# Attention's sink columns copied by another engine, the sums' addition moved the other way, and the last block's remainder behind a later slot

## The chip, the cores and the metric

One NeuronCore of a Trainium2 chip runs the kernel. The metric is the device time of one execution in microseconds. Before the change it is 624.29 us, the median of 3 runs (624.04 to 624.83).

The core has a matrix engine (PE, with its weight loads as PEld), a vector engine (DVE), a scalar engine (ACT), a general engine (POOL, also called GpSimd) and a queue that issues most DMAs (SP). Each engine works through its own instructions in program order and waits on semaphores of the others.

## The reference: what is computed

Three stages follow one another. The first is attention with a window and sinks, for batch 2, 8 heads, 768 positions and 64 columns a head; a position sees the last 128 positions and the first 4 (the sinks):

```python
keep = is_sink | in_window
scores = np.where(keep, scale * q @ k.T, -1e9)
a = np.exp(scores - max(scores))
a = a / (np.sum(a, axis=-1, keepdims=True) + 1e-09)
x = a @ v
```

The second is a layer of 512 to 2048 to 512 with a rational function between its products, the third one of the same size with the square of a ReLU:

```python
h = x @ w_in
P = a[0] + a[1] * h + a[2] * h**2 + a[3] * h**3
Q = 1.0 + abs(b[0]) * abs(h) + abs(b[1]) * h**2
x = (P / (Q + 1e-6)) @ w_out
h = np.maximum(x @ w_in2, 0.0)
out = (h * h) @ w_out2
```

There are 1536 tokens in all. The weights come as 64-bit floats.

## The kernel before, in words

**Attention** goes by blocks of 128 positions: `u` from 0 to 11, six to a batch (`NB`). A block has 4 head pairs, and two steps `m`, each with two pairs; `NM` is 24. `step(m)` writes out by hand, in program order, what every engine does: `scores` (PE's products, then DVE's masked copy L368 and a reduction L375 with its accumulator), `expo` (ACT's exponentials L392, whose accumulators give the row sums `rs`), `trans` (PE transposes the probabilities, ACT copies them from PSUM, POOL splits them into two triangles at L433 and L437), `pv` (PE, into the bank `O`).

The sinks are 8 columns for each head, 64 in a block. In an even step, between the first and the second pair's `scores`, stand `sinks(u - 1)` and `sums(u - 1)`. The first copies these columns from the probabilities `pe` to the tile `sr` (L401, DVE; the first block of a batch, 0 and 6, has none). The second adds 1e-9 to the row sums in place (L408, ACT) and writes their reciprocals to the next 8 columns of `sr` (L409, DVE). `sinks_t` transposes `sr` on PE (L413); in the odd step `sinks_and_sums` multiplies it with the sinks' values (L465) and spreads the reciprocals (L469), and `result` multiplies the block's output with them (L475, DVE, tile `xf`).

`parts_of(u)` splits a finished block into two parts for the layers' products: ACT casts it (`xh`, L482), POOL subtracts (`xl`, L483). It stands two blocks later, in the even step behind the second `scores`; for the last block, 11, it stands at the end of the last step.

**The layers** go by slots. A step `k` of the layers is a chunk of 512 tokens and a piece of 128 of the 2048 columns; `slot(k)` has, in program order, for ACT and POOL the split of step `k - 2` (`act_c`: `gh` at L653, `gl` at L654), the conversion of weights that are ready (`w_fin`, L273 and L274), DVE's rest of step `k - 1` (`act_b`: the cubic L621, which gives a PSUM bank `T` back, ACT's logarithm and exponential L638 and L639, then L642, L644, L646), PE's first product of step `k + 1` (`g1`, L592), ACT's and POOL's start of step `k` (`act_a`, L608 to L613), weight conversion steps until `due(k)` (`w_until`, three DVE instructions a tile: L240, L246, L252), and PE's second product of step `k - 2` (`g2`, L671). Slots 0 and 1 are issued inside `attention`, with the last two steps of attention (24 and 25) between their parts; slots 2 and on by a loop behind it. The last block lies in the third chunk, whose first step is `k = 8`.

The conversion has a scratch bank and a switch: `conv["tag"]` names the PSUM bank, `U` in attention and `O` later, and `conv["on"]` is off from step 24 until attention has been issued. In between, attention's memory pool `ap` is closed and the pool `wp2` for more weights opened in its place; `wpool` says in which pool a weight tile lies.

Tiles that matter here: `sr` has two buffers, `rs` three, `xf` two, the bank `T` two, `O` one.

Of the kernel before, what the change touches and what calls it, by code (L numbers as in the profile page):

```python
# [11 lines left out]
ACTF = mybir.ActivationFunctionType  # L12
ALU = mybir.AluOpType
# [24 lines left out]
def kernel(  # L38
# [13 lines left out]
    nc = tc.nc  # L52
# [4 lines left out]
    NU = B * NB  # L57
# [33 lines left out]
    eps = cst.tile([P, 1], F32, name="eps")  # L91
# [45 lines left out]
    def setup_rest(rel, win, snk, tmp, m_1, m_2, tri):  # L137
        def addm_s(dst, src):
            nc.scalar.activation(out=dst, in_=src, func=ACTF.Identity, scale=BIG, bias=nbig)

        nc.vector.tensor_scalar(out=tri, in0=rel[:, P:], scalar1=0.0, scalar2=None, op0=ALU.is_lt)
        nc.gpsimd.tensor_tensor(out=tmp, in0=win[:, 0:P], in1=win[:, P:], op=ALU.add)
        nc.gpsimd.tensor_tensor(out=win[:, P:P + SK], in0=snk[:, 0:SK], in1=win[:, 0:SK], op=ALU.subtract)
        yield
        addm_s(m_1[:, SK:], tmp)
        nc.scalar.activation(out=win[:, P:P + SK], in_=win[:, P:P + SK], func=ACTF.Relu)
        addm_s(m_1[:, 0:SK], win[:, P:P + SK])
        yield
        addm_s(m_2[:, SK:], tmp)
        addm_s(m_2[:, 0:SK], snk[:, 0:SK])  # L150
# [26 lines left out]
    conv = {"tag": "U", "on": True}  # L177
# [12 lines left out]
    for j, (kind, m) in enumerate(jobs):  # L190
        n = 1 if kind == "v" else 1 + (wtiles[m][::2] == (0, 0)) if kind == "w" else WS + (m >= LATE)
# [73 lines left out]
    def w_fin():  # L265
        m = wst["fin"]
        if m not in wx or len(spare) <= keep[0] or int(spare[0][1:]) >= len(wpool):
            return
        wst["fin"] += 1
        xf = wx.pop(m).bitcast(F32)  # L270
        tag = spare.pop(0)
        t = wpool[int(tag[1:])].tile([P, 2, DM], F32R, tag=tag, name="w")
        nc.scalar.copy(out=t[:, 0], in_=xf)  # L273
        nc.gpsimd.tensor_tensor(out=t[:, 1], in0=xf, in1=t[:, 0].bitcast(F32), op=ALU.subtract)  # L274
        W[wtiles[m]] = (t[:, 0], t[:, 1], tag)
# [9 lines left out]
    def ps_t(tag=None, tail=False):  # L285
        if tail:
            return ps_s()[:, 0]
        if tag is None:
            tag = "U" if hq else "T"
        return ps.tile([P, 512], F32, tag=tag, name=tag, bufs=2 if tag == "T" else 1)  # L290


    def attention(ap, extra):
# [46 lines left out]
        def sink_keys(u):  # L340
            nc.gpsimd.tensor_copy(
                keys[:, :, :, P:], keys[:, :, u % NB, 0:SK].unsqueeze(2).to_broadcast([P, NPR, NB, SK])
            )
# [54 lines left out]
        def sinks(u):  # L398
            t = pe_t.pop(u)
            if u % NB:  # L400
                nc.vector.tensor_copy(  # L401
                    sr[u % 2][:, 0:HS].rearrange("p (r e s) -> p r e s", r=NPR, e=2),
                    t[:, :, :, ROW - BS:ROW - P],
                )

        def sums(u):
            rs = rs_t.pop(u)
            nc.scalar.activation(out=rs, in_=rs, func=ACTF.Identity, bias=eps)  # L408
            nc.vector.reciprocal(out=sr[u % 2][:, HS:HS + H], in_=rs)  # L409

        def sinks_t(u):
# [67 lines left out]
        def parts_of(u):  # L479
            c, t0 = u // UPC, (u % UPC) * P  # L480
            x, h = f.pop(u), xh[c][:, :, t0:t0 + P]
            nc.scalar.copy(out=h, in_=x)  # L482
            nc.gpsimd.tensor_tensor(out=xl[c][:, :, t0:t0 + P], in0=x, in1=h.bitcast(F32), op=ALU.subtract)  # L483

        NM = NU * NPR // 2
# [7 lines left out]
        def fill(d, m):  # L493

            for _ in range(m):
                nc.tensor.matmul(
                    d.rearrange("p (j n) -> p j n", n=P), lhsT=wz,
                    rhs=wz.unsqueeze(1).to_broadcast([P, 4, P]), start=True, stop=True,
                )
# [14 lines left out]
        def step(m):  # L514
            w_fin()
            nonlocal bd, moe, rest, heads
            n, (u, a) = 2 * m, divmod(m, 2)
            if m < NM:
                scores(n)
            if a == 0 and u >= 1:  # L520
                sinks(u - 1)
                sums(u - 1)
            if m < NM:
                scores(n + 1)
                if n in DENSE:
                    fill(ps_t("T"), DENSE[n])
            if m == 0:
                rest = setup_rest(*next(masks), m_1, m_2, tri)
                next(rest)
                sink_keys(0)  # L530
            if a == 0 and 2 <= u <= NU:
                parts_of(u - 2)
            if m < NM:
                expo(n)
            if m in (1, 2):
                next(rest, None)
            if 0 < m <= NM:
                trans(m - 1)
            if m == 1:
                for t in sr:  # L540
                    nc.gpsimd.memset(t, 0.0)
                bd = diagonal()
                heads = bd.rearrange("p h d -> p (h d)")
                moe = setup_moe()
            if a == 0 and u + 2 < NU:
                load(u + 2)
            if a == 0 and m < NM and u % NB == 0:
                load_sinks(u // NB)
            if m >= 5:
                next(moe, None)  # L550
                next(moe, None)
            if a == 1 and u >= 1:
                sinks_and_sums(u - 1)
            if 1 < m:
                pv(m - 2)
            if m < NM:
                expo(n + 1)
            if a == 0 and u >= 1:
                sinks_t(u - 1)
            if m == NM - 1:  # L560
                g1(0)
            if m < NM and a == 1 and u % NB == 0:
                if u:
                    sink_keys(u)
                sink_values(u // NB, bd)
            extra(m)
            if a == 1 and u >= 1:
                result(u - 1)
            if m == NM + 1:
                parts_of(NU - 1)  # L570

        for m in range(NM):
            step(m)
        for j in range(2):
            slot(j, lambda: step(NM + j))


    def part(L, g):
# [21 lines left out]
    def layers(mp, due):  # L600
# [56 lines left out]
        def g2(k):  # L657
            L, g, c, f = steps[k]
            f0, f1 = part(L, g)[0], part(L, g)[1] - 1
            if f == f0:  # L660
                acc[L, g, c] = [t[:, m] for t in [ps_s(), ps_s()] for m in range(2)]
            wo = W[L, f, 1]
            gg = gq.pop(k)
            for m in range(4):
                s = slice(m * P, (m + 1) * P)
                for a, b in ((0, 0), (0, 1), (1, 0)):
                    if L == 0:
                        lh, rh = wo[a][:, s], gg[b]
                    else:
                        lh, rh = gg[a][:, s], wo[b]  # L670
                    nc.tensor.matmul(  # L671
                        acc[L, g, c][m], lhsT=lh, rhs=rh,
                        start=(f == f0 and a + b == 0), stop=(f == f1 and a == 1),
                    )
            if c == NCH - 1:
                w_free((L, f, 1))
            if f == f1:
                done.append((L, g, c))
# [45 lines left out]

        K = len(steps)

        def slot(k, mid=None):
            if 0 <= k - 2:
                act_c(k - 2)
            w_fin()  # L730
            w_fin()
            if 0 <= k - 1 < K:
                act_b(k - 1, lambda: w_until(min(due(k), wst["int"] + 1)))
            if k + 1 < K:
                g1(k + 1)
            if k < K:
                act_a(k)
            if mid:
                cubic(st[k][1], hq[k])
                hq[k] = None  # L740
                mid()
            split_late()
            w_until(due(k))
            if 0 <= k - 2:
                g2(k - 2)
            if k == K + 1:
                finish(0)
                finish(1)
# [253 lines left out]
    EARLY = 2  # L1002
# [19 lines left out]
    slot, slots = layers(mp, due)  # L1022
    with tc.tile_pool(name="ap", bufs=1) as ap:
        NM = NU * NPR // 2

        def extra(m):
            if m == 1:
                for _ in range(NWR):
                    w_load()
            if m % 2:  # L1030
                w_until(min(WS * NA, m - 1))
            if m == NM:
                conv["on"] = False

        attention(ap, extra)
    conv["tag"], conv["on"] = "O", True
    wp2 = main.enter_context(tc.tile_pool(name="wp2", bufs=1))
    wpool += [wp2] * (NW - NA)
    for n in range(EARLY, slots):
        slot(n)  # L1040
        if n == KL + 3 * NF - 3:
            fl = verdict()
# [43 lines left out]
```

## Time and profile before

| what | value |
|---|---|
| median of 3 runs | 624.29 us |
| the profiled execution | 624.6 us |
| its span | 622.9 us |
| PE busy | 609.0 us (98%) |
| DVE busy | 434.4 us (70%) |
| ACT busy | 355.8 us (57%) |
| POOL busy | 329.2 us (53%) |
| granted clock of PE | 0.998 |

The span is what the trace covers; the rest of the execution's time lies around it. An engine's busy time is the time in which one of its instructions was running. PE's ends are modelled, so that a busy PE need not be PE at its peak. Attention lies in the first 85 us of the span, layer 1 follows to about 250 us, then layer 2.

### The profile page before, as it was taken

What the parts mean: (1) busy time and instruction counts of PE and PEld (TensorE: products, weight loads), DVE (VectorE), ACT (ScalarE), POOL (GpSimd) and SP (SyncE); (2) the same over time, 40 slices, a digit from 0 to 9 for tenths busy, and PEclk for the clock granted to TensorE, in tenths of its full rate; (3) what the DMA queues carried; (4) which work ended last, traced back from release to release, by engine and by line L of the source; (5) the groups of instructions that cost most, each with busy time, mean ns of one, the idle gap of its engine ahead of it and who ended that gap; (6) DMA issues with size and microseconds to landing.
All of it is one profiled execution on the core that took longest, in us unless ns stands there. A gap on an engine that the chain in (4) does not pass through costs nothing.

```text
span 622.9 us, 9430 instructions
## 1 busy us (share of the span) xinstructions
PE 609.0 (98%) x3317; PEld 491.1 (79%) x3317; DVE 434.4 (70%) x873; ACT 355.8 (57%) x748; POOL 329.2 (53%) x293
## 2 busy tenths in 40 slices
PE   9999999999999999999999999999999999999995
PEld 6666777788888878888888888888888888888884
DVE  5998957989989889877768879598594422441421
ACT  5999977888886877877869543243332222222210
POOL 4567655777776767666857575444352222222221
PEclk9999999999999999999999999999999999999999
DMA  8857411423332333121111447557365355500102
GB/s 232 244 146 214 120 36 35 128 87 93 98 102 78 97 97 101 38 64 35 35 34 35 115 148 256 192 176 234 131 207 198 116 191 168 175 28 1 67 1 73
DMA packets 64231, 72.03 MB, mean 116 GB/s; under 512 B 15280, under 2 KB 55216, under 8 KB 64176
## 3 DMA queue, kind: packets, MB, share of 16 engines
q1 hardware_dynamic: 64032, 71.35, 37.1%
q8 instruction: 28, 0.46, 0.3%
q14 instruction: 27, 0.22, 0.1%
q10 hardware_dynamic: 144, 0.00, 0.0%
HBM read 68.20 MB, written 3.15 MB: 115 GB/s over the span
## 4 chain that ended last, share of the span: by engine, by line
PE 65%; DVE 19%; ACT 11%; issue 2%; DMA 1%; SPq 0%; DVEq 0%; ACTq 0%
PE s L671 30%; PE T L592 23%; PE U L592 7%; DVE t L646 3%; DVE U L644 3%; ACT U L638 2%; ACT U L639 2%; ACT gh L653 2%; ACT w L273 2%; DVE t L642 2%; DVE wx L252 2%; DVE ns L375 1%; DVE O L240 1%; PE O L453 1%; PE s L363 1%
## 5 line engine op out<-in xcount | busy, mean ns | idle before, releaser
L592 PE MATMUL T<-xh,w 128*128 128x512 f32 x640 | 211.0, 391 | 0.5 <-DVE t L621 0.4
L654 POOL TENSOR_TENSOR gl<-g,gh 128x512 fp32r<-128x512 f32 x48 | 62.2, 1295 | 157.9 <-ACT gh L653 157.8
L592 PEld LDWEIGHTS T<-xh,w 128*128 128x128 f32 x640 | 120.2, 188 | 27.9 <-DVE t L621 2.7
L671 PE MATMUL s<-gh,w 128*128 128x512 f32 x384 | 126.0, 389 | 0.0
L592 PE MATMUL T<-xl,w 128*128 128x512 f32 x320 | 124.6, 389 | 0.0
L671 PE MATMUL s<-w,gh 128*128 128x512 f32 x384 | 118.1, 389 | 0.0
L274 POOL TENSOR_TENSOR w<-wx,w 128x512 fp32r<-128x512 f32 x64 | 82.7, 1293 | 7.2 <-ACT w L273 7.2
L654 POOL TENSOR_TENSOR gl<-t,gh 128x512 fp32r<-128x512 f32 x48 | 62.1, 1294 | 44.6 <-ACT gh L653 43.0
L671 PEld LDWEIGHTS s<-gh,w 128*128 128x128 f32 x384 | 72.1, 188 | 15.0
L671 PEld LDWEIGHTS s<-w,gh 128*128 128x128 f32 x384 | 72.0, 188 | 14.9
L613 POOL TENSOR_TENSOR t<-t,ah 128x512 f32<-128x512 f32 x48 | 62.2, 1296 | 37.7 <-ACT t L610 35.8
L653 ACT CAST gh<-g 128x512 fp32r<-128x512 f32 x48 | 29.9, 623 | 81.8 <-PE s L671 74.5
L671 PE MATMUL s<-gl,w 128*128 128x512 f32 x192 | 74.8, 390 | 0.9 <-POOL gl L654 0.9
L671 PE MATMUL s<-w,gl 128*128 128x512 f32 x192 | 74.7, 389 | 0.0
L592 PEld LDWEIGHTS T<-xl,w 128*128 128x128 f32 x320 | 60.1, 188 | 12.2
L653 ACT CAST gh<-t 128x512 fp32r<-128x512 f32 x48 | 29.9, 622 | 46.2 <-DVE t L646 41.9
L642 DVE SCALAR_TENSOR_TENSOR t<-t,U 128x512 f32<-128x512 f32 x48 | 33.0, 687 | 30.1 <-ACT U L639 29.5
L627 DVE TENSOR_TENSOR g<-r,T 128x512 f32<-128x512 f32 x32 | 21.8, 683 | 41.8 <-ACT r L617 41.5
L617 ACT ACTIVATE r<-T 128x512 f32<-128x512 f32 x32 | 19.2, 600 | 53.2 <-PE T L592 53.1
L392 ACT ACTIVATE pe<-ns,nmax 128x136 f32<-128x136 f32 (+1 forms) x96 | 38.3, 400 | 10.0 <-DVE nmax L375 9.6
L671 PEld LDWEIGHTS s<-gl,w 128*128 128x128 f32 x192 | 36.0, 188 | 8.8 <-POOL gl L654 1.4
L273 ACT CAST w<-wx 128x512 fp32r<-128x512 f32 x64 | 39.3, 615 | 6.4 <-DVE wx L252 6.4
(136 smaller groups left out, 1033.4 us busy)
## 6 DMA issues: line engine op xcount, KB each, us to landing
wr<-in_w_in_dram SPq DMA_DIRECT2D x54, 512.0 KB, 3.7
wr<-in_w_out_dram SPq DMA_DIRECT2D x52, 512.0 KB, 3.7
qr<-in_q_dram SPq DMA_DIRECT2D x12, 256.0 KB, 4.1
keys<-in_k_dram SPq DMA_DIRECT2D x12, 256.0 KB, 4.5
vr<-in_v_dram SPq DMA_DIRECT2D x12, 256.0 KB, 5.6
wr<-in_v_dram SPq DMA_DIRECT2D x6, 512.0 KB, 4.3
out_dram<-part SPq DMA_DIRECT2D x12, 256.0 KB, 2.0
vsc<-in_v_dram SPq DMA_DIRECT2D x2, 16.0 KB
```

Of the source, the lines that this page charges most:

```text
L273: nc.scalar.copy(out=t[:, 0], in_=xf)
L274: nc.gpsimd.tensor_tensor(out=t[:, 1], in0=xf, in1=t[:, 0].bitcast(F32), op=ALU.subtract)
L392: nc.scalar.activation(out=t[:, e, ROW - w:], in_=ns[e][:, 0:w], func=ACTF.Exp, scale=-1.0, bias=nmax[:, ix:ix + 1], accum_out=rs[:, 2 * p ...
L592: nc.tensor.matmul(h, lhsT=wi[a][:, kk * P:(kk + 1) * P], rhs=(xh, xl)[b][c][:, kk, :], start=(kk == 0 and a + b == 0), stop=(kk == KD - 1 ...
L613: nc.gpsimd.tensor_tensor(out=t, in0=t, in1=ah, op=ALU.mult)
L617: nc.scalar.activation(out=r, in_=h, func=ACTF.Relu)
L627: nc.vector.tensor_tensor(out=g, in0=st.pop(k), in1=h, op=ALU.mult)
L642: nc.vector.scalar_tensor_tensor(out=t, in0=t, scalar=QP, in1=r0, op0=ALU.add, op1=ALU.mult)
L644: nc.vector.scalar_tensor_tensor(out=r0, in0=t, scalar=-2.0, in1=r0, op0=ALU.add, op1=ALU.mult)
L653: nc.scalar.copy(out=gh, in_=g)
L654: nc.gpsimd.tensor_tensor(out=gl, in0=g, in1=gh.bitcast(F32), op=ALU.subtract)
L671: nc.tensor.matmul(acc[L, g, c][m], lhsT=lh, rhs=rh, start=(f == f0 and a + b == 0), stop=(f == f1 and a == 1),)
```

## The change

The copy of the sinks' columns is issued on ACT's queue in place of DVE's, the addition to the row sums on DVE's in place of ACT's. The split of block 11 goes from the end of the last step of attention, in slot 1, to the end of slot 2, behind its second product; slot 2 is issued inside `attention` for this, before the pool `ap` is closed. The conversion's tag and switch are set in the last step of attention, for slot 2.

```diff
         def sinks(u):
             t = pe_t.pop(u)
             if u % NB:
-                nc.vector.tensor_copy(
+                nc.scalar.copy(
                     sr[u % 2][:, 0:HS].rearrange("p (r e s) -> p r e s", r=NPR, e=2),
                     t[:, :, :, ROW - BS:ROW - P],
                 )
 
         def sums(u):
             rs = rs_t.pop(u)
-            nc.scalar.activation(out=rs, in_=rs, func=ACTF.Identity, bias=eps)
+            nc.vector.tensor_scalar(out=rs, in0=rs, scalar1=eps, scalar2=None, op0=ALU.add)
             nc.vector.reciprocal(out=sr[u % 2][:, HS:HS + H], in_=rs)
...
             if a == 1 and u >= 1:
                 result(u - 1)
-            if m == NM + 1:
-                parts_of(NU - 1)
 
         for m in range(NM):
             step(m)
         for j in range(2):
             slot(j, lambda: step(NM + j))
+        slot(2, after=lambda: parts_of(NU - 1))
...
-        def slot(k, mid=None):
+        def slot(k, mid=None, after=None):
...
             if 0 <= k - 2:
                 g2(k - 2)
+            if after:
+                after()
...
             if m == NM:
                 conv["on"] = False
+            if m == NM + 1:
+                conv["tag"], conv["on"] = "O", True
 
         attention(ap, extra)
-    conv["tag"], conv["on"] = "O", True
     wp2 = main.enter_context(tc.tile_pool(name="wp2", bufs=1))
     wpool += [wp2] * (NW - NA)
-    for n in range(EARLY, slots):
+    for n in range(EARLY + 1, slots):
         slot(n)
```

## Rows read from the trace of the kernel before

**Rows 1.** The page, engines: busy us, share of the span, instructions.
```profile
PE 609.0 (98%) x3317; PEld 491.1 (79%) x3317; DVE 434.4 (70%) x873; ACT 355.8 (57%) x748; POOL 329.2 (53%) x293
```

**Rows 2.** Busy time by stage: stretch, length, PE, PEld, DVE, ACT, POOL, clock, DMA, GB/s.
```profile
40.00:50.00 10.00, 9.10 (x118) 6.72 (x115) 9.14 (x41) 9.07 (x37) 7.08 (x9) 1.00 0.40 111
```

**Rows 3.** Waits, whole span: who waited for whom, us in total, times, longest.
```profile
PEld T L413 <- DVE sr L409: 5.9, 10, 1.2
...
PE T L413 <- DVE sr L409: 3.4, 6, 1.0
...
PEld T L592 <- DVE t L621: 2.7, 6, 0.6
...
PE s L671 <- POOL gl L654: 0.9, 1, 0.9
```

**Rows 4.** Groups by line, 0 to 140 us: busy us, mean ns | idle before.
```profile
L401 DVE COPY sr<-pe 128x64 f32<-128x64 f32 x10 | 9.2, 917 | 0.0
...
L408 ACT ACTIVATE rs<-rs,eps 128x8 f32<-128x8 f32 x12 | 3.6, 299 | 0.2
...
L415 ACT COPY st<-T 128x128 f32<-128x128 f32 x11 | 2.7, 244 | 0.0
```

**Rows 5.** DVE in order of time, attention: start us, us taken.
```profile
26.53 0.86 DVE L401 COPY sr<-pe 128x64 f32<-128x64 f32 x1
27.32 0.19 DVE L409 RECIPROCAL sr<-rs 128x8 f32<-128x8 f32 x1
...
40.01 1.24 DVE L401 COPY sr<-pe 128x64 f32<-128x64 f32 x1
...
53.40 0.20 DVE L409 RECIPROCAL sr<-rs 128x8 f32<-128x8 f32 x1
...
91.09 0.19 DVE L401 COPY sr<-pe 128x64 f32<-128x64 f32 x1
```

**Rows 6.** POOL in order of time, attention.
```profile
26.06 1.28 POOL L274 TENSOR_TENSOR w<-wx,w 128x512 fp32r<-128x512 f32 x1 [0.96 <-ACT w L273]
27.30 1.27 POOL L483 TENSOR_TENSOR xl<-xf,xh 128x512 fp32r<-128x512 f32 x1
...
39.93 1.27 POOL L483 TENSOR_TENSOR xl<-xf,xh 128x512 fp32r<-128x512 f32 x1 [1.38 <-ACT xh L482]
...
52.78 1.27 POOL L334 TENSOR_TENSOR vm<-bd,vsc 64x512 f32<-64x512 f32 x1 [2.24 <-DMA vsc<-in_v_dram]
54.01 1.27 POOL L274 TENSOR_TENSOR w<-wx,w 128x512 fp32r<-128x512 f32 x1
```

**Rows 7.** Groups by line, 0 to 140 us: DVE's `tensor_scalar` between SBUF tiles.
```profile
L118 DVE TENSOR_SCALAR su<-su 128x256 f32<-128x256 f32 x1 | 0.3, 283 | 0.0
...
L102 DVE TENSOR_SCALAR m<-su 128x128 f32<-128x128 f32 x1 | 0.2, 228 | 0.0
L134 DVE TENSOR_SCALAR su<-su,nw 128x8 f32<-128x8 f32 x1 | 0.2, 224 | 0.0
```

**Rows 8.** One line, L775: shortest/median/longest ns, first and last start us.
```profile
L775 DVE SCALAR_TENSOR_TENSOR bad<-size x1: 1261/1261/1261, 591.4 to 591.4; 128x1 f32<-128x1 f32 x1
```

**Rows 9.** POOL in order of time, layer 2.
```profile
591.32 1.31 POOL L654 TENSOR_TENSOR gl<-g,gh 128x512 fp32r<-128x512 f32 x1 [4.15 <-ACT gh L653]
```

**Rows 10.** DVE in order of time, first slots of layer 1.
```profile
95.13 0.70 DVE L644 SCALAR_TENSOR_TENSOR U<-t,U 128x512 f32<-128x512 f32 x1
95.86 0.75 DVE L646 SCALAR_TENSOR_TENSOR t<-t,fa,U 128x512 f32<-128x512 f32 x1
```

**Rows 11.** ACT in order of time, slots 1 and 2; [idle before <-releaser].
```profile
98.50 0.62 ACT L482 CAST xh<-xf 128x512 fp32r<-128x512 f32 x1 [1.23 <-DVE xf L475]
99.02 0.61 ACT L653 CAST gh<-t 128x512 fp32r<-128x512 f32 x1
```

**Rows 12.** POOL in order of time, slots 1 and 2.
```profile
99.19 1.29 POOL L483 TENSOR_TENSOR xl<-xf,xh 128x512 fp32r<-128x512 f32 x1 [2.18 <-ACT xh L482]
100.44 1.27 POOL L654 TENSOR_TENSOR gl<-t,gh 128x512 fp32r<-128x512 f32 x1
```

## The prediction

> **What bounds the kernel now.** The page first: TensorE (PE) is busy for 98% of the span [rows 1], so from layer 1 on little can be won outside it. Then the table by stage [rows 2]: between 40 and 50 us, in attention, PE, VectorE (DVE) and ScalarE (ACT) are all busy for nine tenths. Then the waits [rows 3]: what PE and its weight loads wait for is the reciprocal of L409 (3.4 us of PE, 5.9 us of loads, ten times), once the remainder `gl` of POOL (0.9 us of PE, ahead of L671), and the cubic of L621, which gives a T bank back (2.7 us of loads). These are the three places that the change can touch. Each block's chain in attention is: DVE's score reductions, the copy of the sinks' columns, the reciprocal, PE's transpose of `sr`, the next scores; DVE works nearly without a gap, so a delay there moves all that follows.
>
> **Why the copy is slow.** The copy of 128x64 takes 0.917 us on average, while ACT copies 128x128 in 0.244 [rows 4]. The lines by time say why [rows 5, 6]. The copy at 26.53 ends at 27.39; POOL's L274 runs from 26.06 to 27.34. The one at 40.01 ends at 41.25; POOL's L483 runs from 39.93 to 41.20. The one at 91.09, at the end of POOL's multiplication, takes 0.19. So the copy itself costs 0.19 and waits until POOL's running instruction has ended, and 0.05 us more.
>
> **The copy moves to ACT, the addition to DVE.** DVE loses ten copies and gets twelve additions over 128x8, in the same place of its queue: behind the reductions, ahead of the reciprocal. The question on which the sum hangs is whether the addition waits for POOL as the copy did. No row has such an addition while POOL works. The bounds: unhindered, the nearest form is L134, a 128x8 `tensor_scalar` with a per-partition scalar, 0.224 us; hindered, it ends where the copy ended. For hindered: L118 and L102 do 256 and 128 elements in 283 and 228 ns, so 128 more cost 55 ns [rows 7]. That is over two elements per ns, a rate that a DVE instruction reading one stream element by element doesn't reach: the 128x512 operations with two inputs cost 0.69 to 0.75 us [rows 10]. `tensor_scalar` between SBUF tiles thus reads through two ports, as a copy does. And smallness doesn't help: L775, one element per partition, took 1.261 us from 591.4 on while POOL ran L654 from 591.32 to 592.63 [rows 8, 9]. I take the hindered end.
>
> The Trainium skill, "SBUF — State Buffer", section "Who interferes with whom", has a rule on this that speaks against this change: copy, cast and `tensor_scalar` can all run in a mode with two ports, one of which is GpSimd's, and whichever of the two engines comes second waits until the other's whole instruction has ended. The copies above agree with it; for a `tensor_scalar` no run here shows it yet. By that rule the sum is the one below; by the 0.224 us alone it would be that of the first rival.
>
> *Full blocks.* Nine copies (blocks 1 to 5 and 7 to 10) stand in the tight part. The addition ends with POOL as the copy did, up to 0.05 us sooner because it is shorter. But the reciprocal now needs the result of the instruction just ahead on its own engine. It used to start at 27.32, 0.07 before the copy ended [rows 5]; one that needs its predecessor's result starts 0.03 after it (L644 ends at 95.83, L646 starts at 95.86) [rows 10]. So 0.10 later, less 0 to 0.05: 0.05 to 0.10 per block, I take 0.08, nine times: **+0.7 us**.
>
> *Block 6.* Blocks 0 and 6 copied nothing, but now add. In block 6 the reciprocal starts at 53.40 [rows 5], while POOL runs L334 from 52.78 to 54.05 [rows 6]. The addition would end at about 54.10, the reciprocal start 0.7 us late, with all of DVE behind it. ACT, co-critical there, saves its 0.3 us. Bounds 0 and 0.73; I take **+0.6 us**. In block 0 the pipeline is still filling and DVE waits for PE: nothing, with a second 0.7 kept for the range; in block 11 PE works on layer 1 meanwhile, which hides it.
>
> *ACT.* Twelve additions of 0.299 go, ten copies of some 0.25 come (L415 is the nearest, 0.244 for twice the columns, from PSUM [rows 4]), in the same place of its queue and with nothing awaited but ACT's own exponentials. No more than before: nothing, bounds -0.05 and +0.05 a block. PE's transpose now waits for two engines; ACT's copy stands ahead of the exponentials, done long before POOL lets the addition go.
>
> **The last block's remainder behind slot 2.** Today ACT's `xh` cast (L482) waits 1.23 us for DVE's `xf` and starts at 98.50, and `gh` of slot 0 stands behind it, at 99.02 [rows 11]. On POOL, L483 runs from 99.19, then L654 from 100.44 to 101.71 [rows 12], and for this `gl` PE waits 0.9 us. With both moved behind slot 2's second product, `gh` can start when ACT is free, at 97.27 (its input was ready at 96.61, the end of L646 [rows 10]); POOL gets it at about 97.9 and is done by 99.2, before PE asks. The stall goes: **-1.0 us** (bounds 0.9, PE's wait [rows 3], and 1.3, the L483 that goes from ahead of `gl`). ACT's logarithm and DVE's chain for slot 1 start some 1.7 us sooner too; against PE's 1.0 that is 0.7 us of lead, so the T banks come back sooner in the next slots: of the 2.7 us of load waits, of which PE shows part, **-0.7 us** (bounds 0 and 1.3). The moved cast (some 0.6) and subtraction (1.3) then stand ahead of slot 3's `gh` and `gl`, which had waited for DVE and are needed a full product later; the block's columns are read by the third chunk only, far behind. The conversions' tag and switch set earlier issue the same steps in slot 2; no DMA changes place, those of the weights follow DVE. The second weight pool opens one slot later than before, and its first tile is written in slot 4: nothing.
>
> **Sum.** +0.7 +0.6 -1.0 -0.7 = -0.4 us. The profiled execution took 624.6 (span 622.9, 1.7 around it), 0.3 above the median of 624.29; against the median the forecast is 623.9.
>
> **The rivals.**
> - *The addition doesn't wait for POOL.* Then the blocks lose the waits that PE shows behind L409: between 3.4 and 5.9 us [rows 3], some of it kept by ACT and PE, which are as busy; I take 4.2 and the tail's 1.7: 618.4. For it: a per-partition scalar may exclude the second port, and L134, too short to tell the rate, is the only row of that form. Against it: rows 5 to 9.
> - *Slower: block 6's addition loses the port twice.* Behind L334 stands L274, ready, another 1.3 us. If POOL's next instruction takes over without a gap, the addition ends 1.9 us late instead of 0.7, and if block 0 pays 0.7 as well, attention loses 0.7+1.9+0.7 = 3.3 against the tail's 1.7: 625.9. It decides from the point where POOL has two instructions back to back. Against it: at 27.3 L483 followed L274 in the same way, and the copy got through between them [rows 5, 6].
> - *The move doesn't pay.* PE finds the next wait (a T bank) in place of `gl`: the tail gives 0.4 and attention's 1.3 stay: 625.2.
>
> **How the numbers follow.** The forecast has 0.60, the free addition 0.24, the port lost twice 0.07, the unpaid move 0.09. A measurement of this kernel tells about 0.2% (1.25 us) from no change. The forecast's own range, from its bounds (-2.2 to +1.4), is 622.1 to 625.7; three twentieths of the whole lie in its part below 623.0, hardly any above 625.5. Faster: 0.24 and 0.11 of the forecast's, 0.35. Slower: 0.07, 0.03 of the unpaid move, 0.04 of the forecast's with block 0 paid in full, 0.14. Same: 0.51. The range for 8 in 10 has to reach the free addition: 618.0 to 625.5.
>
> **What would show it.** In the changed profile: additions (128x8, DVE) of 0.6 to 1.2 us on average, each ending with a POOL instruction, and PE still waiting for L409 for some 3 to 4 us; 0.22 each and that wait gone is the first rival. The block 6 reciprocal about 0.7 us later. `gl` of slot 0 issued near 98 us, no PE wait for it, fewer L592 waits for L621. PE's first product of layer 1 (L592) some 1.3 us later than now. The forecast is wrong if that product starts earlier, or if PE still stalls ahead of its first L671.

## The result, and the profile after

The changed kernel takes 628.62 us, the median of 6 runs (626.14 to 629.18), against 624.27 us before: a ratio of 1.0062, 95% interval 1.0044 to 1.008. It is slower by 4.35 us. The forecast was 623.9, with 618.0 to 625.5 as its range.

Two lines of the page of the changed kernel, to be held against before [rows 1]: PE's share has fallen, and the line of PE's clock, in tenths of full speed over 40 equal slices, which was all nines before, has a dip in the fourth and fifth slice.

```profile
PE 611.7 (97%) x3317; PEld 494.7 (79%) x3317; DVE 437.7 (70%) x875; ACT 355.8 (57%) x746; POOL 329.2 (52%) x293
...
PEclk9998899999999999999999999999999999999999
```

Now DVE in order of time (start us, us taken), to be held against [rows 5]: the additions (L408) in place of the copies, and the products L475 that end a block.

```profile
27.09 0.90 DVE L408 TENSOR_SCALAR rs<-rs,eps 128x8 f32<-128x8 f32 x1
...
40.87 1.22 DVE L408 TENSOR_SCALAR rs<-rs,eps 128x8 f32<-128x8 f32 x1
...
53.02 0.69 DVE L475 TENSOR_TENSOR xf<-O,rb 128x512 f32<-128x512 f32 x1 [0.76 <-PE O L453]
...
54.52 2.40 DVE L408 TENSOR_SCALAR rs<-rs,eps 128x8 f32<-128x8 f32 x1
56.96 0.20 DVE L409 RECIPROCAL sr<-rs 128x8 f32<-128x8 f32 x1
...
63.29 0.69 DVE L475 TENSOR_TENSOR xf<-O,rb 128x512 f32<-128x512 f32 x1 [1.74 <-ACT pe L392]
...
71.94 0.68 DVE L475 TENSOR_TENSOR xf<-O,rb 128x512 f32<-128x512 f32 x1
...
98.23 0.23 DVE L408 TENSOR_SCALAR rs<-rs,eps 128x8 f32<-128x8 f32 x1
```

And POOL in the changed kernel, to be held against [rows 6]:

```profile
26.68 1.28 POOL L274 TENSOR_TENSOR w<-wx,w 128x512 fp32r<-128x512 f32 x1 [0.95 <-ACT w L273]
27.92 1.28 POOL L483 TENSOR_TENSOR xl<-xf,xh 128x512 fp32r<-128x512 f32 x1
...
53.17 1.27 POOL L334 TENSOR_TENSOR vm<-bd,vsc 64x512 f32<-64x512 f32 x1 [1.67 <-DMA vsc<-in_v_dram]
54.41 1.26 POOL L274 TENSOR_TENSOR w<-wx,w 128x512 fp32r<-128x512 f32 x1
55.64 1.25 POOL L483 TENSOR_TENSOR xl<-xf,xh 128x512 fp32r<-128x512 f32 x1
...
97.04 1.30 POOL L612 TENSOR_TENSOR t<-t,ah 128x512 f32<-128x512 f32 x1 [2.22 <-ACT t L609]
```

The addition of 8 columns waits for POOL just as the copy did. The one at 27.09 ends at 27.99, POOL's L274 at 27.96. The one at 98.23 meets only the last 0.11 us of a POOL instruction (L612, which ends at 98.34) and takes 0.23. But in block 6 the addition comes at 54.52, just behind the start of L274 (54.41 to 55.67), and doesn't get through at that one's end: it lasts to 56.92, past the whole of L483 (55.64 to 56.89).

What that does to PE stands in PE's own lines and in the table by stage (stretch, length, PE, PEld, DVE, ACT, POOL, clock, DMA, GB/s) of the changed kernel:

```profile
54.23 0.66 PE L453 MATMUL O<-ph,vr 128*64 128x128 f32 x8
57.22 0.33 PE L413 MATMUL T<-ident,sr 128*128 128x128 f32 x1 [2.33 <-DVE sr L409]
57.48 1.57 PE L363 MATMUL s<-keys,qr 64*64 64x200 f32 x16
```

```profile
50.00:55.00 5.00, 4.88 (x68) 3.59 (x64) 4.17 (x17) 4.64 (x18) 3.33 (x6) 1.00 0.76 196
55.00:60.00 5.00, 2.73 (x21) 1.36 (x21) 4.67 (x16) 2.77 (x12) 1.89 (x2) 0.79 0.66 182
60.00:65.00 5.00, 5.00 (x35) 3.68 (x35) 3.09 (x11) 2.93 (x9) 1.50 (x3) 0.50 0.61 157
65.00:70.00 5.00, 5.00 (x49) 3.61 (x49) 3.33 (x15) 3.01 (x13) 2.20 (x3) 0.68 0.00 0
```

PE stands still for 2.33 us, and then the granted clock falls from 1.00 to 0.50, from 2.4 to 1.2 GHz. From what the three lower rows lack to 1.00, it was at half for (0.21 + 0.50 + 0.32) x 5 / 0.5 = 10.3 us. Then PE is "busy" all the time, but at half the clock.

The blocks' ends in the trace of before, for comparison:

```profile
51.89 0.69 DVE L475 TENSOR_TENSOR xf<-O,rb 128x512 f32<-128x512 f32 x1 [0.76 <-PE O L453]
...
57.83 0.68 DVE L475 TENSOR_TENSOR xf<-O,rb 128x512 f32<-128x512 f32 x1
...
65.04 0.69 DVE L475 TENSOR_TENSOR xf<-O,rb 128x512 f32<-128x512 f32 x1
```

Block 6's stretch takes 63.29 - 53.02 = 10.27 us instead of 5.94, the next one 8.65 instead of 7.21: 5.8 us more in these two.

The other part of the change did what it was forecast to do. In the changed kernel (POOL, then PE, then the waits) slot 0's `gl` (L653 here, L654 before [rows 12]) starts at 105.05, L483 of block 11 comes after it, PE goes from L591 to L670, and from the first product with `gh` to the first with `gl`, without a gap, and the load waits for the T bank are 1.1 us, 2.7 before [rows 3]:

```profile
105.05 1.29 POOL L653 TENSOR_TENSOR gl<-t,gh 128x512 fp32r<-128x512 f32 x1 [0.90 <-POOL t L612]
...
108.81 1.30 POOL L483 TENSOR_TENSOR xl<-xf,xh 128x512 fp32r<-128x512 f32 x1
110.06 1.30 POOL L653 TENSOR_TENSOR gl<-t,gh 128x512 fp32r<-128x512 f32 x1
```

```profile
107.35 0.39 PE L591 MATMUL T<-xh,w 128*128 128x512 f32 x1
107.58 0.39 PE L670 MATMUL s<-gh,w 128*128 128x512 f32 x1
107.81 0.39 PE L670 MATMUL s<-gl,w 128*128 128x512 f32 x1
```

```profile
PEld T L591 <- DVE t L620: 1.1, 3, 0.6
```

### The profile page after: what moved, and what is told of

Read it like the earlier page. It is cut to its first block, busy times and chain, and to the rows that moved or that the text cites. A ratio compares the mean times of both kernels' runs of the same rounds, so it can differ in the third digit from the quotient of the medians.

```text
span 627.5 us, 9443 instructions
## 1 busy us (share of the span) xinstructions
PE 611.7 (97%) x3317; PEld 494.7 (79%) x3317; DVE 437.7 (70%) x875; ACT 355.8 (57%) x746; POOL 329.2 (52%) x293
## 3 DMA queue, kind: packets, MB, share of 16 engines
HBM read 68.20 MB, written 3.15 MB: 114 GB/s over the span
## 4 chain that ended last, share of the span: by engine, by line
PE 84%; DVE 11%; ACT 2%; issue 1%; DMA 1%; SPq 0%; DVEq 0%; ACTq 0%
PE s L670 39%; PE T L591 32%; PE U L591 7%; DVE ns L375 2%; PE s L363 1%; DVE rs L408 1%; PE O L453 1%; DVE s L368 1%; DVE wx L252 1%; PE s L496 1%; DVE xf L475 1%; DVE part L699 1%; DVE t L645 1%; DMA vr<-in_v_dram 1%; PE T L420 1%
## 5 line engine op out<-in xcount | busy, mean ns | idle before, releaser
L591 PE MATMUL T<-xh,w 128*128 128x512 f32 x640 | 210.5, 390 | 0.2 <-DVE t L620 0.2
L653 POOL TENSOR_TENSOR gl<-g,gh 128x512 fp32r<-128x512 f32 x48 | 62.1, 1295 | 157.9 <-ACT gh L652 157.8
L591 PEld LDWEIGHTS T<-xh,w 128*128 128x128 f32 x640 | 120.1, 188 | 26.2 <-DVE t L620 1.1
L670 PE MATMUL s<-gh,w 128*128 128x512 f32 x384 | 126.0, 389 | 0.0
L591 PE MATMUL T<-xl,w 128*128 128x512 f32 x320 | 124.5, 389 | 0.0
L670 PE MATMUL s<-w,gh 128*128 128x512 f32 x384 | 118.3, 389 | 0.0
L274 POOL TENSOR_TENSOR w<-wx,w 128x512 fp32r<-128x512 f32 x64 | 82.7, 1293 | 6.8 <-ACT w L273 6.8
L653 POOL TENSOR_TENSOR gl<-t,gh 128x512 fp32r<-128x512 f32 x48 | 62.2, 1297 | 44.3 <-ACT gh L652 42.6
L670 PEld LDWEIGHTS s<-gh,w 128*128 128x128 f32 x384 | 72.1, 188 | 14.9
L670 PEld LDWEIGHTS s<-w,gh 128*128 128x128 f32 x384 | 72.1, 188 | 15.0
L612 POOL TENSOR_TENSOR t<-t,ah 128x512 f32<-128x512 f32 x48 | 62.2, 1296 | 37.5 <-ACT t L609 35.6
L670 PE MATMUL s<-gl,w 128*128 128x512 f32 x192 | 74.7, 389 | 0.0
L670 PE MATMUL s<-w,gl 128*128 128x512 f32 x192 | 74.7, 389 | 0.0
L591 PEld LDWEIGHTS T<-xl,w 128*128 128x128 f32 x320 | 60.1, 188 | 12.3
L591 PE MATMUL U<-xh,w 128*128 128x512 f32 x128 | 42.1, 390 | 0.0
```

The lines of the kernel that those rows point to most:

```text
L591: nc.tensor.matmul(h, lhsT=wi[a][:, kk * P:(kk + 1) * P], rhs=(xh, xl)[b][c][:, kk, :], start=(kk == 0 and a + b == 0), stop=(kk == KD - 1 ...
L612: nc.gpsimd.tensor_tensor(out=t, in0=t, in1=ah, op=ALU.mult)
L653: nc.gpsimd.tensor_tensor(out=gl, in0=g, in1=gh.bitcast(F32), op=ALU.subtract)
L670: nc.tensor.matmul(acc[L, g, c][m], lhsT=lh, rhs=rh, start=(f == f0 and a + b == 0), stop=(f == f1 and a == 1),)
```

## The experiments

**First set: which part costs, and is it the port?** The theory: the swap loses in attention because the addition waits for POOL's port, the move wins behind it. The rivals put the loss on the move, on ACT, or on the place in DVE's queue.

`swap_alone` is the kernel before with the swap only:

```diff
-                nc.vector.tensor_copy(
+                nc.scalar.copy(
...
-            nc.scalar.activation(out=rs, in_=rs, func=ACTF.Identity, bias=eps)
+            nc.vector.tensor_scalar(out=rs, in0=rs, scalar1=eps, scalar2=None, op0=ALU.add)
```

> The swap of copy and addition without the move of block 11's split. Theory (the swap loses about 7 us in attention, the move wins about 2.5 behind it): 631 us (630 to 632.5), the addition again 0.9 to 1.0 us on average, the longest in block 6 about 2.4, PE's clock at half for some 10 us behind it. Rival (the move is what costs, the swap is neutral): 623.5 to 625.5, clock near 0.998.

Measured: 629.62 us (626.26 to 630.47), before 624.44 in the same session; ratio 1.0075, interval 1.0049 to 1.0101. Addition 1.000 us on average, 2.45 in block 6. The median is 0.4 us under the range that the theory gave and 4 us above the rival's. The swap alone makes the kernel slower.

`move_alone` is the changed kernel with copy and addition back on their engines.

> The move of block 11's split without the swap. Theory: PE's wait of 0.9 us for gl goes and with it most waits for the T bank in the first slots; 621.8 us (621.2 to 622.6), PE's first product of layer 1 at 85.3 us as before. Rival (the move only trades one wait for another): 624 to 625; rival (the move is what costs): 627 to 629.

Measured: 622.44 us (622.09 to 623.07), ratio 0.9969, interval 0.9959 to 0.998. The move is worth 2.0 us. Swap and move together should thus cost 5.2 - 2.0 = 3.2 us where the change cost 4.35; that difference is within the spread of the swapped kernels' runs (4.2 us in `swap_alone`).

`both_on_act` leaves DVE neither:

```diff
-            nc.vector.tensor_scalar(out=rs, in0=rs, scalar1=eps, scalar2=None, op0=ALU.add)
+            nc.scalar.activation(out=rs, in_=rs, func=ACTF.Identity, bias=eps)
```

> The change, but the addition stays on ACT, so that ACT does both and DVE neither. Theory (DVE's wait for POOL's port is the loss, and any DVE instruction there that doesn't use the port is free): the blocks of attention go from 6.65 and 7.2 us to 6.3 to 6.5, where PE and ACT are the limit; 617.5 us (616 to 619.5), clock 0.998. Rival (ACT, as busy as DVE, becomes the limit with ten copies more): 620.5 to 622.

Measured: 616.91 us (616.72 to 617.98), ratio 0.9886, interval 0.987 to 0.9903. This beats both kernels, by 7.5 us the one before. Two stretches of its attention by stage, the columns as above:

```profile
30.00:40.00 10.00, 10.00 (x148) 7.17 (x144) 8.27 (x38) 9.74 (x39) 7.03 (x9) 1.00 0.78 212
40.00:50.00 10.00, 9.94 (x130) 7.59 (x126) 7.48 (x34) 9.71 (x39) 6.52 (x10) 1.00 0.61 152
```

PE hardly has a gap left, where it was busy for 9.10 of 10 us before [rows 2]; DVE has room. ACT at 9.7 of 10 is next, but at this load it does not set the time: the rival's 620.5 is missed by 3.6 us.

`one_port` puts another DVE instruction of the same size into the addition's place; it leaves out the 1e-9, and with it the operand `eps`:

```diff
-            nc.vector.tensor_scalar(out=rs, in0=rs, scalar1=eps, scalar2=None, op0=ALU.add)
+            nc.vector.tensor_reduce(out=rs, in_=rs.unsqueeze(2), axis=AX.X, op=ALU.add)
```

> The change, with the addition replaced by a reduction over one element in the same place, of the same 128x8 and the same operands, before the same reciprocal; the 1e-9 is left out. Theory (the addition waits because tensor_scalar uses the port that POOL uses, a reduction doesn't): 0.15 to 0.25 us each, none longer, 617.5 us (616 to 620), clock 0.998. Rival (any DVE instruction in that place waits, for the row sums or for POOL's order): about 0.9 us each, 627 to 629.

Measured: 616.65 us (616.58 to 616.8), ratio 0.9876, interval 0.9859 to 0.9892. The line of L408 in `one_port` (shortest/median/longest ns, first and last start us):

```profile
L408 DVE TENSOR_REDUCE rs<-rs x12: 151/156/158, 12.6 to 86.0; 128x8 f32<-128x8 f32 x12
```

Same row sums, same place, same reciprocal behind it, and not one of the twelve waits, with POOL at the same work. So neither the place nor the row sums made the addition wait, but its kind of instruction. (An addition without `eps`, the one operand that differs, was not run; but the copies of before have no such operand, and they waited too.) The Trainium skill, "SBUF — State Buffer", section "Who interferes with whom", has it so: `tensor_scalar` can take the port pair that GpSimd uses, `tensor_reduce` never does on this chip. The runs agree with both, with 0.989 us on average for the one and 0.156 for the other.

**Second set: what of the loss is block 6, and what of that is the clock?** `block6_on_act` leaves one addition in twelve on ACT:

```diff
+            if u == NB:
+                nc.scalar.activation(out=rs, in_=rs, func=ACTF.Identity, bias=eps)
+            else:
+                nc.vector.tensor_scalar(out=rs, in0=rs, scalar1=eps, scalar2=None, op0=ALU.add)
```

> The change, with block 6's addition alone left on ACT; the other eleven stay on DVE. Theory (block 6's wait of 2.4 us and the half clock behind it are most of attention's loss; the others lose 0.1 to 0.2 each): 623.2 us (622.4 to 624.2), clock 0.996 to 0.998. Rival (the loss is spread over the blocks, or the half clock comes from elsewhere): 626 to 628.

Measured: 623.32 us (622.57 to 623.95), ratio 0.9981, interval 0.9971 to 0.9991, no run below a mean clock of 0.996. Block 6's addition alone costs 628.62 - 623.32 = 5.3 us. The other eleven and the ten copies on ACT cost the rest, 623.32 - 622.44 = 0.9 us. These medians come from different sessions; with each taken against the kernel before in its own session (624.27, 624.70 and 624.44 us), the two costs are 5.7 and 0.6 us.

`pe_filled` keeps every wait and gives PE work in block 6:

```diff
             sd = ps_t(tail=u == NU - 1)
+            if u == NB:
+                fill(sd, 9)
```

> The change, with nine products of zeros on PE ahead of block 6's transpose, about 2 us of PE work where it waits for the reciprocal; the addition and its wait stay. Theory (PE's idle stretch makes the clock fall, and the fall costs some 3 us by itself): DVE's addition still 2.4 us, clock 1.00 through 55 to 70 us, 625.2 us (624.2 to 626.2), no run at 0.99. Rival (the clock costs nothing, since DVE and ACT set the pace of attention): 627.5 to 629, whatever the clock.

Measured: 625.47 us (624.78 to 626.22), ratio 1.0016, interval 1.0006 to 1.0026, mean clock 0.996 to 0.998 in all ten runs. In `pe_filled`: DVE's addition, PE's products of zeros (L498), and the table by stage.

```profile
54.03 2.29 DVE L408 TENSOR_SCALAR rs<-rs,eps 128x8 f32<-128x8 f32 x1
```

```profile
54.32 2.33 PE L498 MATMUL T<-wz 128*128 128x512 f32 x9
```

```profile
55.00:60.00 5.00, 4.94 (x43) 3.29 (x43) 4.69 (x18) 2.92 (x12) 1.48 (x3) 1.00 0.64 172
60.00:65.00 5.00, 3.92 (x60) 2.43 (x55) 4.73 (x16) 4.02 (x15) 3.53 (x5) 1.00 0.51 129
```

The addition still takes 2.29 us, the clock stays at 1.00, and the kernel is 628.62 - 625.47 = 3.15 us faster for work that computes nothing. So of block 6's 5.3 us the clock is about 3.2 (3.6 against each session's own kernel before) and the wait itself about 2.1, the difference of 625.47 and 623.32, which are of one session.

**Third set: why did the addition lose the port in block 6 only?** Elsewhere, too, L483 follows L274 without a gap, and the addition gets through between them. In block 6 there is L334 ahead, which works on 64 of 128 partitions. `values_later` takes it away from there:

```diff
-                sink_values(u // NB, bd)
+                if u == 0:
+                    sink_values(0, bd)
+            if m == 2 * NB + 3:
+                sink_values(1, bd)
```

> The change, with POOL's multiplication L334 for the second batch (64 of 128 partitions) one block later, so that in block 6 L274 and L483 follow each other without L334 ahead of them. Theory (the addition lost the port between L274 and L483 because of L334 ahead of them; elsewhere it gets through between these two): block 6's addition 0.6 to 1.3 us, PE's wait there at most 1.2, no half clock; 624.0 us (623.2 to 625.2). Rival (in block 6 the order of L274 and L483 alone loses it): 2 us or more and 627 to 629.

Measured: 623.79 us (623.06 to 624.39), ratio 0.9986, interval 0.9976 to 0.9995. In `values_later`, DVE, then POOL:

```profile
54.46 0.62 DVE L408 TENSOR_SCALAR rs<-rs,eps 128x8 f32<-128x8 f32 x1
```

```profile
53.79 1.27 POOL L274 TENSOR_TENSOR w<-wx,w 128x512 fp32r<-128x512 f32 x1 [2.34 <-ACT w L273]
55.02 1.27 POOL L483 TENSOR_TENSOR xl<-xf,xh 128x512 fp32r<-128x512 f32 x1
```

The addition ends at 55.08 with L274 (55.06). So without L334 ahead it gets through. It also came later within L274 here, 0.67 us behind its start and not 0.11; the late runs below show that this isn't what lets it through. Two things could make L334 matter: three POOL instructions in a row, or the half of the partitions. `values_all_rows` loads the values into the other 64 partitions as well and multiplies on 128:

```diff
             nc.sync.dma_start(out=t[0:HS], in_=v[b, :, 0:SK, :])
+            nc.sync.dma_start(out=t[HS:], in_=v[b, :, 0:SK, :])
...
-                out=m[0:HS].rearrange("p (h d) -> p h d", h=H), in0=bd[0:HS],
-                in1=vs[b][0:HS].unsqueeze(1).to_broadcast([HS, H, D]), op=ALU.mult,
+                out=m.rearrange("p (h d) -> p h d", h=H), in0=bd,
+                in1=vs[b].unsqueeze(1).to_broadcast([P, H, D]), op=ALU.mult,
```

> The change, with L334 made to work on all 128 partitions (the values are loaded twice; the second half of its output isn't read), in its old place. Theory (POOL's part for the unused 64 partitions runs ahead by an instruction, so the port is never free between L274 and L483; with all partitions used it is): block 6's addition ends with L274, 1.0 to 1.4 us, no half clock or a short one; 624.8 us (623.8 to 626). Rival (three POOL instructions in a row, whatever their partitions): 2.4 us, 627.5 to 629.5.

Measured: 623.98 us (623.33 to 624.99), ratio 0.9991, interval 0.9982 to 1.0001. The time is as expected, but the profile says that the question wasn't put: here the addition came at 54.13, still in the multiplication (L335 in this kernel, 53.05 to 54.33), and got through at that one's end after 0.23 us. It never met the boundary behind L274.

```profile
54.13 0.23 DVE L409 TENSOR_SCALAR rs<-rs,eps 128x8 f32<-128x8 f32 x1
```

```profile
53.05 1.28 POOL L335 TENSOR_TENSOR vm<-bd,vsc 128x512 f32<-128x512 f32 x1 [1.93 <-DMA vsc<-in_v_dram]
```

So both were run again with the addition made late, by a reduction of zeros ahead of it on DVE, so that it comes in the middle of L274 in either kernel:

```diff
+            if u == NB:
+                nc.vector.tensor_reduce(
+                    out=ap.tile([P, 1], F32, name="late"), in_=wz.bitcast(F32).unsqueeze(1).to_broadcast([P, 4, P]),
+                    axis=AX.XY, op=ALU.add,
+                )
             nc.vector.tensor_scalar(out=rs, in0=rs, scalar1=eps, scalar2=None, op0=ALU.add)
```

> The change, with a reduction over 512 columns of zeros on DVE ahead of block 6's addition, some 0.6 us, so that the addition comes in the middle of L274 and not just behind its start; L334 on 64 partitions as in the change. Theory (behind an L334 on half of the partitions the port isn't free at L274's end, at whatever point of L274 the addition comes): the addition ends with L483, 1.6 to 2.0 us, PE waits over 2 us, half clock behind it; 628 to 630 us. Rival (it lost only because it came within 0.1 us of L274's start): it ends with L274, 0.4 to 0.8 us, 624.5 to 626.

> The same late addition in block 6, with L334 on all 128 partitions. Theory (with all partitions at work POOL's parts stay in step, and the port is free for a moment at L274's end): the addition ends with L274, 0.4 to 1.0 us, no half clock; 624.5 to 626 us. Rival (three POOL instructions in a row keep the port, whatever their partitions): it ends with L483, 1.6 to 2.2 us, 628 to 630.

Measured: `half_rows_late` 627.47 us (625.08 to 628.03), ratio 1.0053, interval 1.0036 to 1.007; `all_rows_late` 624.14 us (623.75 to 625.39), ratio 0.9998, interval 0.9988 to 1.0007. Both lie somewhat (0.4 to 0.5 us) under the ranges expected. The profile of `half_rows_late` is of its quickest run, 625.08 us. The addition (DVE) and POOL's three instructions around it, in `half_rows_late`:

```profile
54.49 1.67 DVE L413 TENSOR_SCALAR rs<-rs,eps 128x8 f32<-128x8 f32 x1
```

```profile
52.41 1.27 POOL L334 TENSOR_TENSOR vm<-bd,vsc 64x512 f32<-64x512 f32 x1 [1.54 <-DMA vsc<-in_v_dram]
53.65 1.27 POOL L274 TENSOR_TENSOR w<-wx,w 128x512 fp32r<-128x512 f32 x1
54.87 1.26 POOL L488 TENSOR_TENSOR xl<-xf,xh 128x512 fp32r<-128x512 f32 x1
```

and in `all_rows_late`:

```profile
54.29 0.74 DVE L414 TENSOR_SCALAR rs<-rs,eps 128x8 f32<-128x8 f32 x1
```

```profile
52.51 1.27 POOL L335 TENSOR_TENSOR vm<-bd,vsc 128x512 f32<-128x512 f32 x1 [1.82 <-DMA vsc<-in_v_dram]
53.74 1.26 POOL L274 TENSOR_TENSOR w<-wx,w 128x512 fp32r<-128x512 f32 x1
54.97 1.27 POOL L489 TENSOR_TENSOR xl<-xf,xh 128x512 fp32r<-128x512 f32 x1
```

With half of the partitions the addition ends at 56.16, with L488 (56.13); with all of them at 55.03, with L274 (55.00). The order of POOL's instructions is the same in both, and the addition comes at the same place within L274 to 0.3 us. So it is the half-filled instruction ahead that decides whether the addition gets the port at the next boundary. In all four traces with L334 on 64 partitions right ahead of L274 the addition didn't: it took 2.40 us in the changed kernel, 2.45 in `swap_alone`, 2.29 in `pe_filled`, 1.67 here. That POOL's part for the empty 64 partitions runs ahead by an instruction is a reading that fits; no row shows the parts themselves, and it stays open.

## Why the prediction was wrong, by its own steps

Full blocks, block 6 and the move were forecast at +0.7, +0.6 and -1.7 us. Measured one by one they are +0.9, +5.3 and -2.0, together 4.2, where the change cost 4.35. The miss is block 6.

- **The addition waits for POOL: right.** It was argued from the copies' ends, from two `tensor_scalar` lengths and from a one-element instruction [rows 5 to 9]; L408 took 0.989 us on average and `one_port` shows the cause. The first rival, the free addition, has fallen for this kernel; its price of 618.4 was near the 616.65 and 616.91 of the two kernels whose DVE doesn't wait.
- **Full blocks, +0.7 us: right in size.** All but block 6's addition, with the copies on ACT, cost 0.9 us (`block6_on_act` against `move_alone`; 0.6 with each against its own session's kernel before). The reciprocal starts behind the addition now: at 56.96, 0.04 after its end.
- **Block 6, +0.6 us: the step that failed.** It read "the addition would end at about 54.10, the reciprocal start 0.7 us late". The cost is 5.3 us. Two things went wrong in it. The prediction put the addition at the time of the old reciprocal, 53.40, within L334. It came at 54.52, 1.12 us later, while L334 came only 0.39 later (53.17 against 52.78). DVE's lateness from the blocks ahead, 0.73 us from block 0's end to block 5's where five times 0.08 was forecast, had not been carried to this place. So the addition came behind L274's start and didn't get the port at L274's end: 2.40 us. Losing the port once more than reckoned was the second rival's mechanism (it had it at L334's end), priced at 1.9 us and given 7 chances in 100; the wait measured 2.1. The argument against it, the copy that got through between L274 and L483 [rows 5, 6], compared two boundaries that differ in what POOL did before: L334's 64 partitions stand in its row, and were not read as meaning anything. And no step asked what PE's clock would do if PE stood still for that long, 2.33 us: 3.15 of the 5.3 us. With it the rival's 625.9 would have been 629, near the 628.62 measured, though the rival also had 0.7 us for block 0 that no run shows.
- **Block 0, nothing: right.** The addition does wait there for POOL, 0.65 us from 13.02 on, but the block doesn't end later for it. The first block's end is 0.4 us later in the changed profile. But POOL's setup at L142, ahead of any changed instruction, is 0.48 later there (8.94 against 8.46), and lies between 8.06 and 8.91 in the first four experiments. Counted from L142, block 0 ends after 9.38 us before and after 9.30 in the changed kernel.
- **ACT, nothing: right.** Ten copies at 0.244 us for twelve additions at 0.299.
- **The move, -1.7 us: right**, -2.0 measured in `move_alone`. Stall and part of the load waits went, as said. How much of the 2.0 is the stall and how much the T bank was not measured apart.

## What to carry to other kernels

A small VectorE instruction is not a cheap one if it may need the port that GpSimd is using: count it as the rest of GpSimd's instruction, or choose a form that doesn't need it (a reduction here took 0.156 us in the place of 0.989) or another engine. Look at what GpSimd runs around each single place of it, and mark instructions on fewer partitions: behind one of these the wait went past the next instruction as well. And a gap in TensorE's work can have a second price in its clock: here one of 2.33 us cost about 3.2 us more. Where a wait can't be avoided, cover the gap with work, as `pe_filled` did.

## What the runs showed that was not expected

- Behind a POOL instruction on 64 partitions, DVE doesn't get the port at the end of the instruction after it: the late addition took 1.67 us, against 0.74 with 128. The Trainium skill, "GPSIMD Engine Reference", section "Instruction dispatch", says that GpSimd's cores each serve 16 partitions and go on to the next instruction as soon as their own share is done, others perhaps still at work. The two late runs agree with that, though they show only the instruction as a whole.
- The half clock isn't of one length. Five runs of the changed kernel show a mean clock of 0.989 or 0.990 and 628.16 us or more; one shows 0.994 and 626.14. In `swap_alone` one run of 626.26 has 0.997, the others (629.6 to 630.47) 0.990 to 0.992. What sets the length wasn't tried, and it stays open.
- Nine products of zeros made the kernel 3.15 us faster.
